# Top-32 attention followed by a SmeLU block: exponentials issued half a step earlier, SmeLU with one read of PSUM, and first products interleaved with the last products of the chunk before

## The chip, the cores and the metric

The kernel runs on one core of a Trainium2 chip. TensorE (PE, with its weight loads as PEld), VectorE (DVE), ScalarE (ACT), GpSimd (POOL) and SyncE (SP, which only issues DMAs here) each work through their own queue of instructions in order, and wait for each other by semaphores. The metric is the device time of one execution in microseconds; lower is better. The kernel before takes 1746.03 us, the median of three runs (1745.57 to 1747.68).

## The reference

All arrays are float32. There are 8 batches, 8 heads, 576 positions and head size 64; the second part has 4608 rows, 512 columns in and out and 2048 hidden columns.

```python
def _attn_ref(q, k, v):
    top_k = 32
    scores = scale * np.matmul(q, k.transpose(0, 1, 3, 2))
    kth = np.partition(scores, -top_k, axis=-1)[..., -top_k:-top_k + 1]
    scores = np.where(scores >= kth, scores, -1000000000.0)
    scores = scores - np.max(scores, axis=-1, keepdims=True)
    attn = np.exp(scores)
    attn = attn / (np.sum(attn, axis=-1, keepdims=True) + 1e-09)
    return np.matmul(attn, v)

def _moe_ref(x, w_in, w_out):          # x: attention output, (B*S, H*D)
    h = x @ w_in
    g = np.where(h >= 1, h, np.where(h <= -1, 0.0, (h + 1) ** 2 / 4.0))
    return g @ w_out
```

## The kernel before

**Steps.** The attention is cut into 144 steps. A step takes 128 query rows for a pair of heads, both held side by side as `[128, 2, 576]` (index `i` below is the head of the pair). In a step:

- `begin` (line 555) has PE make the scores into four PSUM tiles `sp` (line 258), and ACT copies them, scaled, to `s` (line 261). `s` has three buffers.
- `pairs` (line 266): DVE makes `more`, the larger of each score in the first half and its partner in the second, 288 wide.
- `weights` (line 271) finds the 32nd largest score. It is a generator: each `next` emits the instructions up to the next `yield`. DVE takes the eight largest of `more` (`max`, line 283) and strikes them out (`match_replace`, line 292), four times over. After the first eight, ACT forms `nmax`, minus the row maximum, and two exponentials `e` (line 287), one a head. Then DVE handles the smaller partners (lines 297 to 304), makes `more` of the next step (line 309), and masks `e` against the threshold while summing it to `z` (line 312). The reciprocal `rz` (line 318) ends DVE's part, and POOL scales `e` by it (line 325). During the conversion of the weights (the early phase) PE does that scaling with a diagonal matrix instead. `e` has two buffers.
- `transpose_w` (line 333): PE transposes `e` into PSUM and ACT copies it to `wT` (lines 345 and 353). This is one step after the weights were found.
- `values` (line 356): PE multiplies with v, and ACT copies the result into `xT`, the input of the second part. This is another step later.

**Second part.** The 4608 rows form chunks of one or two tiles of 128 rows. For each chunk and each of 16 blocks `f` of 128 hidden columns, `hidden` (line 391) has PE make four accumulating products `ph` (line 394), 128 columns wide for one tile or 256 for two, and the SmeLU gives `g`. In the common path (lines 398 and 412 to 415) ACT reads `ph` twice, `r = Relu(0.5 h + 0.5)` and `g = Relu(h - 1)`, and POOL forms `min(r, 1)`, squares it and adds `g`. There are two buffers of `r`, sixteen of `g`, and three PSUM tiles with the tag `ph`, which `values` uses too. Then `final` (line 417) makes the second products two blocks at a time for one tile into `py` (line 422), and after the last of them ACT copies `py` to `y`, which a DMA writes out. `py` and `y` have one buffer each. The first four chunks of the program handle each tile by itself (128 wide); from the fifth on both tiles go together, where a chunk has two. The last chunk has its own path through DVE (lines 402 to 406).

**Order.** The program writes the order of PE, DVE, ACT and POOL by hand (`tc.manual_schedule`): each engine's instructions stand in the order in which the Python code emits them. The loop at line 605 runs over the steps. In iteration m it emits the values of step m-2 and the scores of step m+2, and then seven slots. `parts` (line 615) says how many `next` of the weights of step m fall into each slot; the transposes of step m-1 come at the end of slot 2 (slot 1 in the early phase); and every slot ends with `advance` (line 501), which emits products of the second part from the queue `pending`, so many that they are spread evenly: `share` (line 611) is the smaller of what is left per step left and what is queued per step until the next chunk is due. The counts are in units of one 128-column product; a `hidden` of two tiles and a pair of `final` count 8 each.

When a chunk's rows are ready, `values_until` (line 587) puts its 16 `hidden` behind what is queued, and its `final` pairs behind those. A second run of the whole program, without the pairing, stands behind a branch that isn't taken here.

## Time and profile before

| | |
|---|---|
| median of three runs | 1746.03 us (1745.57 to 1747.68) |
| the profiled execution | 1746.35 us |
| its span | 1744.5 us |
| mean granted TensorE clock | 0.982 |
| PE matmuls `ph` (line 394) | 3200 records, 558.0 us busy |
| PE matmuls `py` (line 422) | 1152 records, 530.9 us busy |
| DVE maxima (line 283), strikes (line 292) | 465.4 and 375.6 us busy |
| ACT exponentials (line 287) | 288, 213.4 us busy |
| ACT reads of `ph` (lines 398 and 412) | 400 and 368, 166.5 and 153.6 us busy |
| POOL on the products (lines 413, 414, 415) | 173.2, 213.9 and 255.9 us busy |

One matmul of the program is two records in the trace. "Busy" counts the time in which an engine executes at least one instruction; matmuls overlap, so a busy PE isn't necessarily at its fastest, and the distance between the starts of two matmuls that follow each other closely is the better measure of what one costs. A wait in brackets, `[2.00 <-ACT g L412]`, is the idle time of the engine just before the instruction and what ended it. Steps can be counted on DVE by their one reciprocal (line 318).

### The profile page before, as it was taken

The numbers are of one execution on the slowest core, as the hardware profiler recorded it, in microseconds if no ns is written. First come the engines' busy times: TensorE is split into PE (matmuls) and PEld (weight loads), VectorE is DVE, ScalarE is ACT, GpSimd is POOL, SyncE is SP. The second block draws the span as 40 slices with busy tenths as digits, with TensorE's granted clock in tenths as the row PEclk, the third lists the DMA queues.
The fourth block names the chain that finished last, engine by engine and source line by source line (L and its number), as shares of the span: only waits on it lengthen the run. The fifth ranks groups of instructions, "written<-read, shape, count | busy, mean of one in ns | idle before, by whom it ended". The sixth has DMA issues, their size and how long they took to land.

```text
span 1744.5 us, 33535 instructions
## 1 busy us (share of the span) xinstructions
PE 1639.4 (94%) x10665; PEld 1151.5 (66%) x10665; DVE 1537.0 (88%) x4875; ACT 1083.2 (62%) x2942; POOL 946.9 (54%) x1668
## 2 busy tenths in 40 slices
PE   5588989999999999999999999999999999999998
PEld 4476575667766757476756767567667666666665
DVE  7999979888899999999987999999997998899752
ACT  6688575676667857576655647556555555466452
POOL 5689183665544817264646645436365554555550
PEclk7799999999999999999999999999999999999999
DMA  8333112111121112111200101000010000000000
GB/s 253 116 98 97 46 30 65 44 43 41 42 63 52 44 49 65 46 49 41 62 13 22 25 22 44 17 24 17 23 39 19 19 10 14 13 7 7 7 7 15
DMA packets 116668, 74.63 MB, mean 43 GB/s; under 512 B 87296, under 2 KB 95488, under 8 KB 116480
## 3 DMA queue, kind: packets, MB, share of 16 engines
q1 hardware_dynamic: 116480, 72.37, 14.5%
q8 instruction: 87, 1.43, 0.3%
q14 instruction: 101, 0.83, 0.2%
HBM read 62.91 MB, written 9.44 MB: 41 GB/s over the span
## 4 chain that ended last, share of the span: by engine, by line
PE 65%; DVE 14%; POOL 11%; ACT 6%; issue 3%; DMA 0%; POOLq 0%; DVEq 0%; SPq 0%; ACTq 0%
PE py L422 25%; PE ph L394 18%; PE sp L258 7%; PE po L364 7%; PE pw L344 5%; DVE tops L283 4%; DVE more L292 3%; POOL g L415 3%; POOL r L414 3%; DVE e L312 3%; POOL e L325 2%; POOL r L413 2%; ACT s L261 1%; DVE seconds L300 1%; ACT r L398 1%
## 5 line engine op out<-in xcount | busy, mean ns | idle before, releaser
L394 PE MATMUL ph<-xT,w_in 128*128 128x128 f32 (+1 forms) x3200 | 558.0, 326 | 14.4 <-ACT g L412 13.2
L422 PE MATMUL py<-w_out,g 128*128 128x512 f32 x1152 | 530.9, 600 | 2.0 <-ACT y L426 2.0
L394 PEld LDWEIGHTS ph<-xT,w_in 128*128 128x128 f32 x3200 | 472.3, 192 | 87.9 <-ACT g L412 26.0
L325 POOL TENSOR_SCALAR e<-e,rz 128x576 f32<-128x576 f32 x264 | 195.0, 750 | 520.2 <-DVE rz L318 488.8
L283 DVE MAX8 tops<-more 128x8 f32<-128x288 f32 x1152 | 465.4, 445 | 0.0
L292 DVE MATCH_REPLACE8 more<-tops,more 128x288 f32<-128x288 f32 x864 | 375.6, 442 | 0.0
L422 PEld LDWEIGHTS py<-w_out,g 128*128 128x128 f32 x1152 | 205.2, 190 | 224.1 <-issue 215.8
L312 DVE SCALAR_TENSOR_TENSOR e<-s,kth,e 128x576 f32<-128x576 f32 x288 | 245.7, 881 | 116.6 <-ACT e L287 116.3
L398 ACT ACTIVATE r<-ph,half 128x128 f32<-128x128 f32 (+1 forms) x400 | 166.5, 416 | 216.8 <-POOL g L415 156.7
L415 POOL TENSOR_TENSOR g<-r,g 128x128 f32<-128x128 f32 (+1 forms) x384 | 255.9, 666 | 30.2
L413 POOL TENSOR_SCALAR r<-r 128x128 f32<-128x128 f32 (+1 forms) x368 | 173.2, 471 | 132.0 <-ACT r L398 131.7
L414 POOL TENSOR_TENSOR r<-r 128x128 f32<-128x128 f32 (+1 forms) x368 | 213.9, 581 | 30.7
L261 ACT ACTIVATE s<-sp 128x288 f32<-128x288 f32 x576 | 195.2, 421 | 56.8 <-PE sp L258 36.8
L287 ACT ACTIVATE e<-s,nmax 128x576 f32<-128x576 f32 x288 | 213.4, 770 | 7.7
L364 PEld LDWEIGHTS po<-wT,v_in 128*64 128x64 f32 x2048 | 111.8, 137 | 87.9 <-issue 53.2
L258 PE MATMUL sp<-kT,qT 64*128 64x288 f32 x1024 | 163.9, 437 | 4.2 <-ACT kT L218 2.3
L364 PE MATMUL po<-wT,v_in 128*64 128x128 f32 x2048 | 145.5, 280 | 18.7 <-ACT g L412 11.3
L345 ACT COPY wT<-pw 128x512 f32<-128x512 f32 x288 | 154.0, 589 | 13.1 <-PE pw L344 10.6
L344 PEld LDWEIGHTS pw<-ident,e 128*128 128x128 f32 x1056 | 122.2, 142 | 60.0 <-issue 24.4
L344 PE MATMUL pw<-ident,e 128*128 128x128 f32 x1056 | 141.0, 276 | 16.2 <-ACT s L261 10.4
L377 ACT COPY xT<-po 128x128 f32<-128x128 f32 x128 | 34.1, 266 | 195.8 <-PE po L364 195.5
L412 ACT ACTIVATE g<-ph,minus 128x128 f32<-128x128 f32 (+1 forms) x368 | 153.6, 417 | 0.0
(91 smaller groups left out, 1595.1 us busy)
## 6 DMA issues: line engine op xcount, KB each, us to landing
raw<-in_moe_w_out_dram SPq DMA_DIRECT2D x64, 256.0 KB, 2.6
raw<-in_moe_w_in_dram SPq DMA_DIRECT2D x36, 256.0 KB, 2.7
k_in<-in_k_dram SPq DMA_DIRECT2D x64, 128.0 KB, 2.9
q_in<-in_q_dram SPq DMA_DIRECT2D x32, 256.0 KB, 3.1
v_in<-in_v_dram SPq DMA_DIRECT2D x8, 1024.0 KB, 5.8
out_dram<-y SPq DMA_DIRECT2D x32, 256.0 KB, 2.3
kT<-in_moe_w_in_dram SPq DMA_DIRECT2D x16, 256.0 KB, 4.0
v_in<-in_moe_w_in_dram SPq DMA_DIRECT2D x12, 256.0 KB, 4.5
```

Source lines behind the costliest of these rows:

```text
L258: nc.tensor.matmul(o[:, a0 - c0:a1 - c0], qT[d, g, :], kT[d, g, k0:k0 + a1 - a0], start=True, stop=True)
L283: nc.vector.max(out=tops[:, i, r:r + 8], in_=src[:, i, :])
L287: nc.scalar.activation(e[:, i, :], s[:, i, :], AF.Exp, bias=nmax[:, i:i + 1])
L292: nc.vector.match_replace(out=rest[:, i, :], in_to_replace=tops[:, i, r:r + 8], in_values=src[:, i, :], imm_value=LOWEST)
L312: nc.vector.scalar_tensor_tensor(out=e[:, i, :], in0=s[:, i, :], scalar=last[:, i:i + 1], in1=e[:, i, :], op0=ALU.is_ge, op1=ALU.mult, acc ...
L325: nc.gpsimd.tensor_scalar(e[:, i, :], e[:, i, :], rz[:, i:i + 1], 1.0, ALU.mult, ALU.mult)
L344: nc.tensor.transpose(pt[:, c, :], w_in_place, ident)
L364: nc.tensor.matmul(po[j * D:(j + 1) * D], v_in[:, h, c, :] if c < NT else v_tl[0][:, h, :], wT[:, j, c, :] if c < NT else wTt, start=(c == ...
L394: nc.tensor.matmul(ph, w_in[:, kk, f * P:(f + 1) * P], xT[:, kk, c0:c1], start=(kk == 0), stop=(kk == NK - 1))
L414: nc.gpsimd.tensor_tensor(out=r, in0=r, in1=r, op=ALU.mult)
L415: nc.gpsimd.tensor_tensor(out=g, in0=r, in1=g, op=ALU.add)
L422: nc.tensor.matmul(py, gs[f][:, i * P:(i + 1) * P], w_out[:, f, :], start=(f == 0), stop=(f == NF - 1))
```

## The change

Three things change.

1. `pairs`, the first `max`, `nmax` and the exponentials move out of a step's own `weights` into `first_top`, which the step before calls after its last strike and ahead of its last `max`. `weights` of step m therefore begins with a strike and holds the start of step m+1. `parts` is changed to the new count of yields.
2. In the common path of `hidden`, ACT reads `ph` once: `u = Relu(h + 1)` into `g`. POOL forms `c = min(u / 2, 1)` into `r`, then `u - c`, then `c (u - c)`, both in place in `g`. (For u up to 2 this is u²/4, and above it u - 1, which is h.) The path of the last chunk and the path of odd `f` during the conversion keep their operations.
3. From the fifth chunk on, when a chunk becomes ready, up to eight of the last `final` pairs in the queue are taken out and put back with the new chunk's `hidden` spread behind each of them: two `hidden` a pair when there are eight. So that there are such pairs, `share` leaves 64 units in the queue while the next step belongs to a chunk of that kind with two tiles.

```diff
-        def weights(st, after):
-            s, m = st["s"], st["m"]
-            tops = att.tile([P, 2, TOP_K + 8], F32, name="tops", bufs=3)
+        def first_top(st):
+            s = st["s"]
+            if paired:
+                pairs(st)
+            st["tops"] = tops = att.tile([P, 2, TOP_K + 8], F32, name="tops", bufs=3)
             st["e"] = e = att.tile([P, 2, S], F32, name="e")
             nmax = att.tile([P, 2], F32, name="nmax")
+            for i in range(2):
+                nc.vector.max(out=tops[:, i, 0:8], in_=(st["more"] if paired else s)[:, i, :])
+            nc.scalar.activation(nmax, tops[:, :, 0], AF.Copy, scale=-1.0)
+            for i in range(2):
+                nc.scalar.activation(e[:, i, :], s[:, i, :], AF.Exp, bias=nmax[:, i:i + 1])
+                yield
+
+        def weights(st, after):
+            s, m, tops, e = st["s"], st["m"], st["tops"], st["e"]
...
-            for r in range(0, TOP_K, 8):
+            for r in range(8, TOP_K, 8):
+                for i in range(2):
+                    nc.vector.match_replace(out=rest[:, i, :], in_to_replace=tops[:, i, r - 8:r],
+                                            in_values=src[:, i, :], imm_value=LOWEST)
+                src = rest
+                if r == 8:
+                    yield
+                if r + 8 == TOP_K:
+                    yield
+                    yield from first_top(after) if after is not None else (None, None)
                 for i in range(2):
                     nc.vector.max(out=tops[:, i, r:r + 8], in_=src[:, i, :])
-                if r == 0:
-                    nc.scalar.activation(nmax, tops[:, :, 0], AF.Copy, scale=-1.0)
-                    for i in range(2):
-                        nc.scalar.activation(e[:, i, :], s[:, i, :], AF.Exp, bias=nmax[:, i:i + 1])
-                        if i == 0:
-                            yield
-                if r + 8 < TOP_K:
-                    for i in range(2):
-                        nc.vector.match_replace(out=rest[:, i, :], in_to_replace=tops[:, i, r:r + 8],
-                                                in_values=src[:, i, :], imm_value=LOWEST)
-                    src = rest
-                yield
...
-            if paired and after is not None:
-                pairs(after)
...
                 else:
-                    nc.scalar.activation(g, ph, AF.Relu, bias=minus, scale=1.0)
-                    nc.gpsimd.tensor_scalar(r, r, 1.0, 0.0, ALU.min, ALU.max)
-                    nc.gpsimd.tensor_tensor(out=r, in0=r, in1=r, op=ALU.mult)
-                nc.gpsimd.tensor_tensor(out=g, in0=r, in1=g, op=ALU.add)
+                    nc.scalar.activation(g, ph, AF.Relu, bias=one)
+                    nc.gpsimd.tensor_scalar(r, g, 0.5, 1.0, ALU.mult, ALU.min)
+                    nc.gpsimd.tensor_tensor(out=g, in0=g, in1=r, op=ALU.subtract)
+                    nc.gpsimd.tensor_tensor(out=g, in0=g, in1=r, op=ALU.mult)
...
-                    pending.extend(hiddens(i0, i1) + rest + [work for i in range(i0, i1) for work in finals(i)])
+                    new = hiddens(i0, i1)
+                    if i0 == 0 and ch >= EARLY_CHUNKS:
+                        places = []
+                        while pending and not pending[-1][3] and len(places) < NF // 2:
+                            places.append(pending.pop())
+                        for x, work in enumerate(reversed(places)):
+                            pending.append(work)
+                            upto = (x + 1) * NF // len(places)
+                            pending.extend(new[x * NF // len(places):upto])
+                        new = [] if places else new
+                    pending.extend(new + rest + [work for i in range(i0, i1) for work in finals(i)])
...
-            share = min((total - spent) / (n + 2 - m), sum(work[0] for work in pending) / coming)
+            next_chunk = steps[m][3] if m < n else 0
+            keep = NF * DM // P if next_chunk >= EARLY_CHUNKS and len(chunks[next_chunk]) == 2 else 0
+            behind = sum(work[0] for work in pending) - keep
+            share = min((total - spent) / (n + 2 - m), max(behind, 0) / coming)
...
-                parts = [1] * SLOTS if early else [1, 2, 2, 2, 0, 0, 0]
+                parts = [1] * SLOTS if early else [1, 1, 2, 2, 1, 0, 0]
```

PE's transposes of `e` stay as they are. No matmul, DVE instruction or DMA is added or removed.

## The prediction

> **What bounds the kernel now.** I read the page first (its busy row), then busy time by stage, then the waits of the whole run and of each stage, then one crowded step in order of time.
>
> ```profile
> PE 1639.4 (94%) x10665; PEld 1151.5 (66%) x10665; DVE 1537.0 (88%) x4875; ACT 1083.2 (62%) x2942; POOL 946.9 (54%) x1668
> ```
>
> Two engines are near full, and neither is full all the time. Busy time by stage (the window in us, its length, then each engine) shows that they take turns:
>
> ```profile
> 160.00:345.00 185.00, 172.47 (x1199) 119.71 (x1198) 160.19 (x519) 119.57 (x352) 103.04 (x212) 1.00 0.17 51
> 345.00:510.00 165.00, 157.39 (x1162) 113.19 (x1162) 140.80 (x460) 108.95 (x324) 87.81 (x188) 0.99 0.17 48
> 510.00:895.00 385.00, 372.45 (x2371) 259.56 (x2370) 373.17 (x1191) 266.23 (x733) 212.11 (x347) 1.00 0.17 48
> 895.00:1062.00 167.00, 163.45 (x991) 110.08 (x990) 143.53 (x457) 93.57 (x239) 76.21 (x137) 1.00 0.09 22
> 1252.00:1531.00 279.00, 276.69 (x1772) 193.21 (x1771) 241.87 (x762) 159.98 (x405) 156.62 (x261) 0.99 0.07 18
> 1605.00:1692.00 87.00, 83.11 (x493) 59.09 (x492) 63.04 (x198) 42.34 (x114) 55.16 (x100) 1.00 0.02 7
> ```
>
> DVE is full in 510-895 (97%); PE is in 1252-1531 (99%); in 160-510 neither is. The waits say why (who waited for whom: us, times, longest):
>
> ```profile
> ACT r L398 <- POOL g L415: 156.7, 113, 6.4
> POOL r L413 <- ACT r L398: 131.7, 46, 10.0
> DVE e L312 <- ACT e L287: 116.3, 80, 6.3
> ```
>
> DVE's only large wait is for the exponentials. Asked by stage, that row is 41.1 us in 160-510, 1.9 in 510-895, 19.6 in 895-1062, 0.7 in 1062-1252, 30.6 in 1252-1531 and 22.3 after 1605: it lies where DVE is not full. One crowded step, from the timeline:
>
> ```profile
> 322.14 1.09 PE L364 MATMUL po<-wT,v_in 128*64 128x128 f32 x16 [2.00 <-ACT g L412]
> ...
> 321.47 0.37 ACT L398 ACTIVATE r<-ph,half 128x128 f32<-128x128 f32 x1 [2.30 <-POOL g L415]
> 321.73 0.36 ACT L412 ACTIVATE g<-ph,minus 128x128 f32<-128x128 f32 x1
> 323.14 0.37 ACT L398 ACTIVATE r<-ph,half 128x128 f32<-128x128 f32 x1 [1.05 <-POOL g L415]
> ...
> 326.55 0.78 ACT L287 ACTIVATE e<-s,nmax 128x576 f32<-128x576 f32 x1
> ...
> 327.36 0.82 DVE L312 SCALAR_TENSOR_TENSOR e<-s,kth,e 128x576 f32<-128x576 f32 x1 [4.56 <-ACT e L287]
> ```
>
> One chain stops three engines. ACT writes `r` into one of two buffers, so it may not be more than two products ahead of POOL; POOL needs about 1.3 us a product (its adds into `g` begin at 323.93, 325.21 and 326.49); ACT stands, PE stands behind the PSUM tile (2.00 us), and the exponential queued behind on ACT makes DVE stand (4.56 us).
>
> **Floors.** A DVE step without POOL work lasts 10.18 us (reciprocals at 1210.61 and 1220.79). PE issues a 512-column `py` every 0.429 us (12 in 5.15 on the chain), a 256-column `ph` every 0.216 (16 in 3.46), a 128-column one every 0.112 (128 in 14.29). The step 1312.3-1324.5 has PE busy throughout and 20 to 21 `py` (8.6-9.0 us), so attention costs PE 3.2-3.6 us a step; I take 3.5. In 160-510 (30 steps, 256 `py`, 817 narrow `ph`) PE needs 109.8 + 91.5 + 105 = 306 us and DVE 305 plus what POOL costs it; the stage lasts 350. So some 40 us are lost to the chain above. In 895-1062 PE needs 60.5 + 31.1 + 14.3 + 49 = 155 of 167 (141 `py`, 144 wide and 128 narrow `ph`, 14 steps); in 1252-1531 it is 87.1 + 80.8 + 14.3 + 84 = 266 of 279 (203, 374, 128, 24 steps).
>
> **The change part by part.**
>
> *smelu.* Outside the last chunk and the odd `f` of the weight-conversion phase, 368 products lose one ACT read of PSUM: 192 narrow at 369 ns and 176 wide at 470 ns, 154 us of ACT. ACT is no bound (62%), so the relief alone is worth nothing. What counts is that ACT no longer writes `r`: its one `Relu` goes to `g`, which has 16 buffers. The wait of ACT for POOL (156.7 us) has nothing left to wait for. What is late next is POOL itself: it still does three operations a product, and the squaring (697 ns wide, 475 narrow) becomes an operation of two tensors like the add (817, 539), so 176 x 0.12 + 192 x 0.064 = 33 us more POOL work. That stays beside other work while POOL's lag is under the time between an `e` scaling and its transposes. In a step of eight narrow products POOL needs 8 x 1.47 + 1.7 = 13.5 us against DVE's 11, a lag of 2.5 us; the products of three such steps, 16 x 1.47 + 3 x 1.7 = 29 us, fit in 33. So POOL isn't a bound over three steps.
>
> *Exponentials sooner.* `first_top` puts `pairs`, the first maxima, `nmax` and both exponentials of step m+1 before the last maxima of step m: no instruction is added. Before, DVE stood as soon as ACT was some 4 us late; now the exponentials have a whole step, about 10 us. That covers the longest wait seen, 6.3 us, so I let the row of 116.3 us go; what appears instead is PE, where PE is the bound.
>
> *A wait added.* `e` has two buffers, and in the new order ACT's exponential of m+1 stands ahead of the copies of m-1's transposes, so it waits for PE's transposes of m-1, and before that `nmax` waits for DVE's maxima, some 6 us into the step. Behind it on ACT: two `wT` copies, the `Relu` of slots 2 to 6, `y` copies; PE waits for those only after three PSUM tiles, 3 x 1.73 = 5.2 us. ACT resumes at about 6.3 + 0.2 + 1.5 + 1.5 = 9.5 us of the step; PE's transposes end about 5 to 7 us into it (in the step begun at 1210.9, the copies that follow them start at 1218.15). I take nothing; between 0 and 0.5 us on some 100 steps (0 and +50).
>
> *Interleaving and the reserve.* From the fifth chunk on, a chunk's 16 wide products go two by two between the last eight `final` pairs of the chunk before. PE's instructions are the same in number. DVE loses to POOL wherever both work: `more` takes 740 ns in 605-646 and 1052 in 1177-1200, the masking 813 and 1051. The same work is spread over more steps, and `pairs` moves to where POOL is busy: +4, between -8 and +15. `keep` holds 64 units back, and in the orders of both programs the changed one has issued 13.7 us fewer products up to the transposes of step 124. They were taken from a stretch where DVE is the bound (steps 36-43) and fall into the last 20 steps, where PE mostly is: +12, between +5 and +14.
>
> *DMAs.* None is added. With the interleaved `final` pairs the copies of `y` and their output DMAs (median 2.3 us to landing) come later on ACT's and SP's queues, past loads of keys, queries and weight pieces, which have whole steps of cover; DMA is 1 to 3 tenths busy after the start. Nothing; were that cover gone, 2 to 3 us at each of 32 outputs' landings that something waits for, of which `y`'s rows show 0.7 us.
>
> The page "SBUF — State Buffer", section "Who interferes with whom", of the Trainium skill speaks against the change: a VectorE instruction with two SBUF inputs and a GpSimd one that reads SBUF exclude each other for the whole instruction. The rows show +0.31 us for `more`, not a whole 0.73 us POOL operation. By the rule some 85 steps of `pairs` would cost +0.73 each where 16 us are paid now, about +46 instead of +4.
>
> **Sum.** Stage 160-510: of 40 us lost, 24 come back (DVE's waits there are 41.1, but POOL's 13.5 us steps keep some; between 8 and 38). 895-1062 and 1252-1531: 25 us above PE's need, half of it, 12 (0 to 25). Where PE's stages meet DVE's, DVE may now be some 7 us further ahead; three such changes, and part of it, 6 (0 to 20). Early stage (30-160: DVE busy 128.2 of 130), 510-895 and the tail after 1692: nothing, since DVE's own work, then the last chunk's unchanged path, fill them (-3 to +3). -24 - 12 - 6 + 12 + 4 = -26 on the profiled span of 1744.5, 1718.5; the execution took 1746.35, 1.85 more than its span, and stands 0.3 over the median 1746.03. So 1720.
>
> **Rivals.** *Much faster*: the chain is undone wholly and the regimes average out; 38 + 25 + 20 saved against 12 + 4: 1679 to 1700. For: PE's and DVE's needs in 160-510 are near 306. Against: uneven steps remain, some with 12 us of products. *Smaller gain or none*: POOL paces 160-510 all the same (busy 13.5 us of the crowded steps), only 8 come back there and 6 elsewhere, and the 12 come late: 1736 to 1750. For: POOL's row of 131.7 us waiting for ACT is small beside its work in these steps. *Slower*: ACT's new hold stalls PE. Its place is the `Relu` and `y` copies behind the exponential; it decides from the point where PE's transposes end earlier than 9.5 - 5.2 = 4.3 us into a DVE step. At 0.2 us a step over 130 steps (26 us) the gain is gone; at 0.5, 65 - 26 gives 1785. Against: a PE that falls behind by 2 us no longer meets the hold, as DVE is then ahead.
>
> **How the numbers follow.** Forecast with 1700 to 1736: 0.58; much faster 0.12; smaller gain (1736 to 1742.5) 0.12; no change, within 0.2% (3.5 us, what a measurement of this kernel can tell) 0.06; slower 0.12. Faster 0.82, same 0.06, slower 0.12. The range runs from 1692, inside the much faster case, to 1747, and leaves out some 0.05 below and 0.14 above. The forecast's own range is 1700 to 1736.
>
> **What would show it.** Right: no row of ACT waiting for POOL's `g`; DVE's wait for `e` under 20 us; ACT near 930 us busy, POOL near 980; the stage up to step 40 shorter by 20 us or more; the last 20 steps longer by some 10. Wrong: PE's waits for ACT's `g`, `y` or `wT` growing by tens of us with ACT standing at `nmax` or `e`; PE waiting for POOL's `e`; DVE steps without products over 10.3 us.

## The result, and the profile after

The changed kernel takes 1756.5 us, the median of four runs (1755.72 to 1758.43), beside 1746.04 us (1745.57 to 1747.68) for the kernel before on the same chip. The ratio is 1.006, with a 95% interval of 1.0042 to 1.0077: slower by 0.6%, where the prediction had 1720 and faster. The profiled execution has a span of 1756.6 us. The busy row of its page:

```profile
PE 1646.4 (94%) x10665; PEld 1161.7 (66%) x10665; DVE 1580.9 (90%) x4875; ACT 974.0 (55%) x2574; POOL 1196.7 (68%) x1669
```

ACT was to be near 930 us and is at 974; POOL was to be near 980 and is at 1197. The groups of POOL's instructions, with shapes kept apart (count, then busy us, mean ns of one, idle before and what ended it), say where that is. Before:

```profile
L413 POOL TENSOR_SCALAR r<-r 128x256 f32<-128x256 f32 x176 | 98.6, 560 | 65.1 <-ACT r L398 64.8
L413 POOL TENSOR_SCALAR r<-r 128x128 f32<-128x128 f32 x192 | 74.6, 389 | 66.9 <-ACT r L398 66.9
```

After:

```profile
L424 POOL TENSOR_SCALAR r<-g 128x256 f32<-128x256 f32 x176 | 210.3, 1195 | 98.9 <-ACT g L423 70.4 <-ACT nmax L283 21.3 <-PE py L433 7.1
L425 POOL TENSOR_TENSOR g<-g,r 128x256 f32<-128x256 f32 x176 | 146.5, 833 | 14.7
L426 POOL TENSOR_TENSOR g<-g,r 128x256 f32<-128x256 f32 x176 | 159.1, 904 | 13.8
L424 POOL TENSOR_SCALAR r<-g 128x128 f32<-128x128 f32 x192 | 142.7, 743 | 105.3 <-ACT g L423 87.9 <-ACT nmax L283 17.5
```

The clamp is an operation of the same kind on the same shape, and takes twice as long: 1195 ns in place of 560, 743 in place of 389. That is 179.8 us more on POOL. A wide product now costs POOL 1.19 + 0.83 + 0.90 = 2.93 us (2.07 before), a narrow one 1.81 (1.40).

The stages in the windows of before:

```profile
160.00:345.00 185.00, 170.62 (x1198) 121.36 (x1198) 167.46 (x529) 108.01 (x303) 116.89 (x198) 0.97 0.18 52
345.00:510.00 165.00, 152.73 (x1117) 109.67 (x1113) 142.20 (x444) 95.73 (x270) 125.78 (x210) 0.98 0.16 45
...
895.00:1062.00 167.00, 167.00 (x1035) 114.48 (x1033) 161.85 (x494) 86.54 (x218) 122.81 (x161) 1.00 0.08 22
1252.00:1531.00 279.00, 277.26 (x1795) 194.51 (x1793) 259.42 (x787) 137.81 (x341) 211.16 (x263) 1.00 0.07 19
```

In 160-510, where a gain of 24 us was expected, PE is now less busy than before (323 us of 350 against 330). In 895-1062 PE and DVE are busier together than before (167 and 162 against 163 and 144): that stage did improve. The waits of the whole run:

```profile
POOL e L335 <- DVE rz L328: 188.0, 44, 8.9
...
POOL r L424 <- ACT g L423: 158.3, 46, 13.6
ACT nmax L283 <- DVE tops L282: 154.0, 61, 5.3
...
ACT e L285 <- PE pwt L362: 102.6, 72, 7.8
...
DVE more L271 <- ACT s L263: 48.3, 25, 7.0
PEld pw L354 <- POOL e L335: 46.5, 39, 6.2
```

The two rows that the prediction wanted gone are all but gone: of ACT's waits for POOL's `g`, 156.7 us at the reads of `ph` before, 3.9 us are left there (in the path that keeps its operations) and 9.0 stand at the exponentials, and DVE waits for the exponentials 5.0 us in place of 116.3. Three came in their place. PE's weight loads wait for POOL's scaled `e`, ACT's exponential waits for PE's transposes, and DVE waits for ACT's scores. In the timeline they follow one another (start, length, engine, line; the wait in brackets):

```profile
278.38 1.47 POOL L335 TENSOR_SCALAR e<-e,rz 128x576 f32<-128x576 f32 x2
279.18 1.97 PE L354 MATMUL pw<-ident,e 128*128 128x128 f32 x8 [6.01 <-POOL e L335]
...
280.94 0.42 PE L362 MATMUL pwt<-ident,e 128*128 128x128 f32 x1
...
281.48 1.44 ACT L285 ACTIVATE e<-s,nmax 128x576 f32<-128x576 f32 x2 [7.82 <-PE pwt L362]
...
291.62 0.76 DVE L271 TENSOR_TENSOR more<-s 128x576 f32<-128x576 f32 x1 [3.04 <-ACT s L263]
```

POOL comes to the scaling of `e` late, behind its products; PE stands 6.0 us until it is done; ACT stands 7.8 us at the next exponential, because one of the two `e` is still being transposed. Some 10 us later DVE stands 3.0 us, waiting for ACT's scores.

Where the time went, step range by step range: the time between the reciprocals of DVE (one a step), summed, and from the last reciprocal to the end of the span. Rows named by what they are; they are explained below.

| us | 0-10 | 11-39 | 40-75 | 76-89 | 90-107 | 108-130 | 131-143 | rest | span |
|---|---|---|---|---|---|---|---|---|---|
| before | 160.5 | 347.2 | 385.0 | 168.7 | 191.0 | 278.5 | 161.1 | 52.5 | 1744.5 |
| after | 166.7 | 346.9 | 394.8 | 155.0 | 197.8 | 270.1 | 159.0 | 66.5 | 1756.6 |
| after, fast clamp | 164.6 | 327.6 | 388.0 | 154.6 | 195.1 | 275.1 | 159.6 | 62.9 | 1727.6 |
| after, no reserve | 166.9 | 348.3 | 398.5 | 169.7 | 200.0 | 289.0 | 159.8 | 63.0 | 1795.2 |
| before, slow clamp | 162.2 | 360.5 | 403.8 | 172.2 | 198.5 | 299.9 | 167.4 | 63.7 | 1828.2 |
| before, fast clamp | 160.7 | 328.7 | 389.6 | 160.8 | 194.6 | 270.3 | 154.8 | 57.6 | 1717.1 |
| 16-bit c | 160.2 | 336.4 | 383.8 | 162.9 | 191.6 | 271.0 | 158.3 | 53.1 | 1717.1 |
| 16-bit c, spread | 160.2 | 336.6 | 382.3 | 162.1 | 191.6 | 271.2 | 152.3 | 52.3 | 1708.6 |
| 16-bit c, spread, sooner | 163.5 | 333.7 | 388.1 | 158.3 | 196.4 | 265.1 | 153.8 | 61.5 | 1720.4 |
| the same, `pairs` earlier | 163.5 | 334.6 | 383.4 | 160.6 | 192.5 | 265.7 | 153.1 | 61.3 | 1714.7 |

From before to after, steps 76-89 and 108-130 gave 22.1 us; steps 0-10, 40-75, 90-107 and the rest lost 6.2 + 9.8 + 6.8 + 14.0. Steps 11-39 gave nothing.

This table counts at DVE, and where the exponentials come sooner DVE runs further ahead of PE: from its last reciprocal to PE's last transpose `pwt` it is 6.9 us before and 20.3 after. So time moves from one of its columns to another without being won or lost. The order of PE's transposes was not changed. Counted from the start of one step's `pwt` to that of another, and from the last one to the end, the same traces give:

| us | 0-10 | 11-39 | 40-75 | 76-89 | 90-107 | 108-130 | 131-143 | rest |
|---|---|---|---|---|---|---|---|---|
| before | 163.8 | 349.6 | 388.6 | 167.0 | 194.5 | 275.0 | 160.2 | 45.8 |
| after | 169.1 | 352.0 | 392.1 | 162.1 | 193.5 | 274.5 | 167.0 | 46.3 |
| after, fast clamp | 167.0 | 330.6 | 391.3 | 162.1 | 192.4 | 274.5 | 164.8 | 45.0 |
| the same, no reserve | 167.0 | 336.5 | 387.6 | 163.9 | 192.4 | 272.4 | 153.1 | 44.9 |
| before, fast clamp | 163.8 | 330.6 | 389.8 | 163.0 | 193.5 | 271.4 | 158.5 | 46.5 |
| 16-bit c | 163.4 | 338.5 | 385.1 | 163.8 | 190.7 | 271.8 | 158.0 | 45.8 |
| 16-bit c, spread | 163.5 | 337.0 | 385.3 | 163.1 | 190.5 | 272.4 | 151.7 | 45.0 |
| 16-bit c, spread, sooner | 166.0 | 342.3 | 386.0 | 163.9 | 191.3 | 272.4 | 153.4 | 45.2 |
| the same, `pairs` earlier | 166.0 | 342.7 | 383.4 | 163.9 | 188.0 | 272.4 | 153.3 | 44.9 |

Here steps 76-89 and 108-130 gave 5.4 us from before to after, steps 0-10, 11-39, 40-75 and 131-143 lost 5.3 + 2.4 + 3.5 + 6.8, and the time after the last transpose stayed (45.8 and 46.3).

### The profile page after: what moved, and what is told of

It reads as the page before. It is cut to its first block, busy times and chain, and to the rows that moved or that the text cites. A ratio compares the mean times of both kernels' runs of the same rounds, so it can differ in the third digit from the quotient of the medians.

```text
span 1756.6 us, 32761 instructions
## 1 busy us (share of the span) xinstructions
PE 1646.4 (94%) x10665; PEld 1161.7 (66%) x10665; DVE 1580.9 (90%) x4875; ACT 974.0 (55%) x2574; POOL 1196.7 (68%) x1669
## 4 chain that ended last, share of the span: by engine, by line
PE 48%; DVE 33%; POOL 11%; issue 5%; ACT 2%; DMA 1%; DVEq 0%; POOLq 0%; ACTq 0%
PE py L433 18%; PE ph L404 14%; DVE more L298 8%; DVE tops L307 7%; PE sp L260 5%; PE po L374 5%; POOL r L424 4%; DVE e L322 4%; PE pw L354 4%; POOL g L426 3%; DVE seconds L312 3%; DVE more L309 3%; POOL g L425 3%; DVE more L271 2%; DVE tops L282 2%
## 5 line engine op out<-in xcount | busy, mean ns | idle before, releaser
L433 PE MATMUL py<-w_out,g 128*128 128x512 f32 x1152 | 541.1, 603 | 4.6 <-ACT y L437 4.6
L404 PEld LDWEIGHTS ph<-xT,w_in 128*128 128x128 f32 x3200 | 478.2, 193 | 101.4 <-issue 54.7
L424 POOL TENSOR_SCALAR r<-g 128x128 f32<-128x128 f32 (+1 forms) x368 | 353.0, 959 | 204.2 <-ACT g L423 158.3
L307 DVE MAX8 tops<-more 128x8 f32<-128x288 f32 x864 | 349.1, 445 | 0.0
L335 POOL TENSOR_SCALAR e<-e,rz 128x576 f32<-128x576 f32 x264 | 205.8, 790 | 206.7 <-DVE rz L328 188.0
L433 PEld LDWEIGHTS py<-w_out,g 128*128 128x128 f32 x1152 | 205.7, 192 | 207.9 <-issue 194.3
L426 POOL TENSOR_TENSOR g<-g,r 128x128 f32<-128x128 f32 (+1 forms) x368 | 265.4, 721 | 28.8
L285 ACT ACTIVATE e<-s,nmax 128x576 f32<-128x576 f32 x288 | 208.8, 768 | 126.1 <-PE pwt L362 102.6
L425 POOL TENSOR_TENSOR g<-g,r 128x128 f32<-128x128 f32 (+1 forms) x368 | 244.6, 665 | 30.7
L322 DVE SCALAR_TENSOR_TENSOR e<-s,kth,e 128x576 f32<-128x576 f32 x288 | 255.8, 925 | 9.9 <-ACT e L285 5.0
L423 ACT ACTIVATE g<-ph,one 128x128 f32<-128x128 f32 (+1 forms) x368 | 151.5, 425 | 182.4 <-PE ph L404 181.9
L263 ACT ACTIVATE s<-sp 128x288 f32<-128x288 f32 x576 | 195.1, 416 | 57.1 <-PE sp L260 51.2
L354 PEld LDWEIGHTS pw<-ident,e 128*128 128x128 f32 x1056 | 122.1, 142 | 76.5 <-POOL e L335 46.5
L271 DVE TENSOR_TENSOR more<-s 128x576 f32<-128x576 f32 x144 | 120.1, 834 | 48.4 <-ACT s L263 48.3
L312 DVE MAX8 seconds<-more 128x8 f32<-128x288 f32 x288 | 118.3, 452 | 20.3 <-POOL excess L337 6.6
```

The costliest lines, as they stand in the source:

```text
L285: nc.scalar.activation(e[:, i, :], s[:, i, :], AF.Exp, bias=nmax[:, i:i + 1])
L307: nc.vector.max(out=tops[:, i, r:r + 8], in_=src[:, i, :])
L322: nc.vector.scalar_tensor_tensor(out=e[:, i, :], in0=s[:, i, :], scalar=last[:, i:i + 1], in1=e[:, i, :], op0=ALU.is_ge, op1=ALU.mult, acc ...
L354: nc.tensor.transpose(pt[:, c, :], w_in_place, ident)
L404: nc.tensor.matmul(ph, w_in[:, kk, f * P:(f + 1) * P], xT[:, kk, c0:c1], start=(kk == 0), stop=(kk == NK - 1))
L424: nc.gpsimd.tensor_scalar(r, g, 0.5, 1.0, ALU.mult, ALU.min)
```

## The experiments

Each time stands beside the kernel before on the same chip, which took 1744.4 to 1746.0 us (medians). In the texts on record, Theory A is that GpSimd's new pair of operations is slow by itself, B that the other tile or contention makes it slow, C that VectorE's own new order and the products put off carry the loss.

### What makes the clamp slow

```diff
-                    nc.gpsimd.tensor_scalar(r, g, 0.5, 1.0, ALU.mult, ALU.min)
+                    (one of eight pairs of operations, by f % 8, the rest as changed)
```

> The changed kernel, but POOL's tensor_scalar from g to r takes one of eight pairs of operations, by f modulo 8 (0: times 0.5, min 1, as changed; 1: min 2, times 0.5; 2: min 2, max 0; 3: times 0.5, times 1; 4: min 2 alone; 5: times 0.5 alone; 6: max 0, min 2; 7: times 0.5, max 0), so most of its g are other numbers. Theory A (the pair of operations sets POOL's speed, not the other tile or the traffic): 0 stays at the 1195 ns wide and 743 narrow that the changed kernel shows, and at least 2 comes near the 560 and 389 of the old pair min, max. Theory B (reading g and writing r, or more contention with DVE, is what costs): all eight lie within 15% of each other, near 1195 and 743.

One run, 1742.2 us. The groups of its `TENSOR_SCALAR`, 128x256 alone. L425 is mult 0.5 then min 1, L427 min 2 then mult 0.5, L433 min alone, L435 mult alone, L429 min 2 then max 0, L431 mult 0.5 then mult 1:

```profile
L427 POOL TENSOR_SCALAR r<-g 128x256 f32<-128x256 f32 x22 | 27.1, 1231 | 4.5 <-ACT g L423 4.1 <-ACT nmax L283 0.4
...
L425 POOL TENSOR_SCALAR r<-g 128x256 f32<-128x256 f32 x22 | 24.8, 1127 | 72.0 <-ACT g L423 52.2 <-ACT nmax L283 19.8
...
L435 POOL TENSOR_SCALAR r<-g 128x256 f32<-128x256 f32 x22 | 21.0, 955 | 15.7 <-ACT g L423 14.3 <-ACT nmax L283 1.5
L433 POOL TENSOR_SCALAR r<-g 128x256 f32<-128x256 f32 x22 | 19.3, 877 | 10.5 <-ACT nmax L283 8.5 <-ACT g L423 2.0
...
L431 POOL TENSOR_SCALAR r<-g 128x256 f32<-128x256 f32 x22 | 11.5, 523 | 13.5 <-ACT g L423 13.5
L429 POOL TENSOR_SCALAR r<-g 128x256 f32<-128x256 f32 x22 | 11.3, 515 | 2.8 <-ACT g L423 2.8
```

Same tiles, same neighbours, same engine: only the pair differs. (These are means, and they include waits for the neighbours; the shortest ones, on 128x128, are 286 to 292 ns for the two fast pairs, 521 and 524 for one operation alone, and 637 to 647 for the other pairs.) Min then max, and mult then mult, take 515 and 523 ns; every other pair tried (max then min too, 1163) takes 1127 to 1328, and even one operation alone takes 877 or 955. Theory A holds and B falls. The kernel before has a fast pair in its clamp (min 1, max 0).

The price of that in the changed kernel, with the clamp made min(u, 1) by the fast pair. Every kernel with this "fast clamp" leaves out the half, so it computes another function; the instructions and their order stay:

```diff
-                    nc.gpsimd.tensor_scalar(r, g, 0.5, 1.0, ALU.mult, ALU.min)
+                    nc.gpsimd.tensor_scalar(r, g, 1.0, 0.0, ALU.min, ALU.max)
```

> The changed kernel with POOL's old pair of operations, min 1 and max 0, from g to r: c becomes min(u, 1) and the output differs; all instructions and their order stay. Theory A (the slow POOL operation ate the gain, 180 us of POOL): 1756.5 falls by 15 to 30, to 1727 to 1742. Theory C (DVE's own order, 0.26 us a step, and the products put off are the loss): within 5 us of 1756.5. POOL's busy time falls from 1197 to about 1010 in both.

1729.35 us (1727.65 to 1732.5), ratio 0.9921 (0.9904 to 0.9937); POOL 989 us busy. So the slow pair costs the changed kernel some 24 to 27 us (by the ratios and by the times) and turns a gain into a loss. Steps 11-39 shrink from 346.9 to 327.6 us, 19.6 below the 347.2 of before: most of the prediction's 24 us are there, and 19.3 of them hung on this operation.

### The parts one by one

VectorE's own order: `pairs` of the next step moved ahead of the last strike, so that the first maxima no longer follow it at once.

```diff
             for r in range(8, TOP_K, 8):
+                if paired and r + 8 == TOP_K and after is not None:
+                    pairs(after)
                 for i in range(2):
                     nc.vector.match_replace(
```

> The changed kernel with the pairs of the next step one instruction group earlier on DVE, ahead of the last strike instead of behind it, so that the first maxima don't follow directly on the pairs they read. Theory C (a DVE instruction that reads what the one just before it wrote waits some 0.13 us, and the new order has two such places a step more): the step without POOL work falls from 10.44 to 10.31, and the time by 8 to 15 us, as more than half of the 144 steps are DVE's. Theory A alone: the step falls as well, but the time by less than 5, since POOL and PE pace the rest.

1753.97 us (1749.95 to 1754.22), ratio 1.006 (1.0043 to 1.0077), the same ratio as the changed kernel. The floor of a step without products went from 10.44 to 10.30 us as Theory C said, and steps 40-75 from 394.8 to 391.4, so the effect is real; it is too small to carry the loss, and far from the 8 to 15 us of Theory C.

The change with the old SmeLU (two reads, squaring) put back:

```diff
-                    nc.scalar.activation(g, ph, AF.Relu, bias=one)
-                    nc.gpsimd.tensor_scalar(r, g, 0.5, 1.0, ALU.mult, ALU.min)
-                    nc.gpsimd.tensor_tensor(out=g, in0=g, in1=r, op=ALU.subtract)
-                    nc.gpsimd.tensor_tensor(out=g, in0=g, in1=r, op=ALU.mult)
+                    (the five lines of before)
```

> The changed kernel with the old SmeLU (two ACT reads, min and max, square, add): the sooner exponentials and the interleaving alone. Theory A (the new SmeLU costs more than it gives): faster than the changed kernel, 1735 to 1750. Theory C: the old SmeLU's hold of ACT by POOL comes back on top of DVE's slower step and the products put off: 1756 to 1775.

1744.43 us (1742.57 to 1745.61), ratio 1.0 (0.9991 to 1.001). Without the new SmeLU the rest of the change is worth nothing, though DVE's wait for the exponentials is gone there as well: it waits 78.8 us for the scores instead.

The other way round, the kernel before with the new SmeLU alone, slow and fast:

> The kernel before with the new smelu alone (one PSUM read, then mult 0.5 and min 1 in one GpSimd operation, subtract, mult); exponentials and order of products as before. Theory A (the new smelu carries the loss through its slow GpSimd operation, whatever the order): 1752 to 1768 us, GpSimd near 1200 us busy. Rival F (the slow operation hurts only because the sooner exponentials make GpSimd's scalings of e urgent): 1742 to 1748 us, as before.

> The kernel before with the one-read smelu whose clamp is the fast pair (c = min(u, 1), output differs); exponentials and order of products as before. Theory A with the prediction's mechanism (ScalarE freed of the two buffers of r is the gain, mostly): 1726 to 1734 us, ScalarE's wait for GpSimd gone, VectorE's wait for the exponentials under 60 us. Rival H (the gain needs the exponentials half a step sooner as well, since a block of products still stands ahead of them): 1738 to 1746 us, with VectorE's wait for the exponentials near the 116 us of before.

Slow: 1831.93 us (1830.36 to 1834.96), ratio 1.0506 (1.0489 to 1.0524), far above what Theory A had written down. Fast: 1720.01 (1719.43 to 1721.36), ratio 0.9862 (0.9845 to 0.9878), better than Theory A's 1726 to 1734; DVE's wait for the exponentials is 61.2 us. The one-read SmeLU by itself, with a fast clamp, gives all that was forecast of the whole change, and one pair of operations moves that kernel by 112 us, over four times what it moves the changed kernel. What happens in the slow one, from its timeline:

```profile
1462.17 1.07 POOL L416 TENSOR_SCALAR r<-g 128x256 f32<-128x256 f32 x1
1463.33 1.17 POOL L417 TENSOR_TENSOR g<-g,r 128x256 f32<-128x256 f32 x1
1464.58 1.12 POOL L418 TENSOR_TENSOR g<-g,r 128x256 f32<-128x256 f32 x1
1465.68 1.47 POOL L327 TENSOR_SCALAR e<-e,rz 128x576 f32<-128x576 f32 x2
...
1478.50 1.47 POOL L327 TENSOR_SCALAR e<-e,rz 128x576 f32<-128x576 f32 x2
...
1466.48 1.85 PE L346 MATMUL pw<-ident,e 128*128 128x128 f32 x8 [3.36 <-POOL e L327]
...
1467.51 0.59 ACT L347 COPY wT<-pw 128x512 f32<-128x512 f32 x1 [3.48 <-PE pw L346]
...
1479.24 1.34 DVE L314 SCALAR_TENSOR_TENSOR e<-s,kth,e 128x576 f32<-128x576 f32 x1 [4.75 <-ACT e L289]
```

POOL runs without a gap, takes 2.6 to 3.5 us a product, and comes to `e` when PE's transposes are already due: PE stands, ACT stands behind PE, and by the next step DVE stands behind ACT. With four wide products in a step (4 x 2.81 us by the means of this kernel, and 1.6 for `e`) POOL needs 12.8 us, which is also the distance of its two scalings of `e` above (1465.68 and 1478.50). In the kernel before, most steps with four wide products last 11.37 or 11.38 us. With the fast clamp POOL needs 10.4. The pair lifts POOL over the length of a step, and from there on POOL sets the pace.

Is it that time as such, or something else the slow pair does? The fast clamp, done twice:

```diff
                     nc.gpsimd.tensor_scalar(r, g, 1.0, 0.0, ALU.min, ALU.max)
+                    nc.gpsimd.tensor_scalar(r, r, 1.0, 0.0, ALU.min, ALU.max)
```

> The kernel before with the one-read smelu and the fast clamp (c = min(u, 1), output differs), the clamp done twice, the second time from r to r: one more fast GpSimd operation a product, about 560 ns wide and 390 narrow, against the 635 and 354 by which the slow pair is longer. With one clamp it took 1720.0 us, with the slow pair 1831.9. Theory N (GpSimd's time as such is what costs, by pacing the crowded steps): 1800 to 1840 us. Rival O (the slow operation does something beyond its own time, to VectorE or to ScalarE): 1725 to 1770 us.

1830.84 us (1829.96 to 1832.29), ratio 1.0485 (1.0469 to 1.0501): the same loss with two fast operations, 515 + 472 ns wide and 380 + 349 narrow:

```profile
L416 POOL TENSOR_SCALAR r<-g 128x256 f32<-128x256 f32 x176 | 90.6, 515 | 71.7 <-ACT g L415 71.7
L417 POOL TENSOR_SCALAR r<-r 128x256 f32<-128x256 f32 x176 | 83.0, 472 | 14.8
```

It is POOL's time. Theory N holds.

Why then does the changed kernel lose only 10 us? Its reserve and its spreading taken out, first with the fast clamp, then with the slow one as changed:

```diff
-            keep = NF * DM // P if next_chunk >= EARLY_CHUNKS and len(chunks[next_chunk]) == 2 else 0
+            keep = 0
```

```diff
-                    if i0 == 0 and ch >= EARLY_CHUNKS:
+                    if False:
```

> The changed kernel with c = min(u, 1) through the fast pair (min 1, max 0), so its output differs, and without the reserve: keep = 0, so that products are handed out as in the kernel before. To be compared with the same kernel with the reserve, 1729.35 us, whose end after the last reciprocal was 62.9 us long against 52.5 us before the change. Theory D (the reserve puts products off into the last steps, where TensorE is the bound, and costs what the prediction said, 5 to 14 us): 1715 to 1724 us; the end back at 53 to 57 us. Rival E (the products put off come out of steps where VectorE is the bound, so that what the end gains those steps lose, or the long end has another cause): 1726 to 1733 us.

> The same kernel (c = min(u, 1), output differs, keep = 0) and also without the spreading of a chunk's first products among the last ones of the chunk before: they are queued in one block again. Theory D holds the spreading for nearly free of cost: within 4 us of the kernel that only loses the reserve. Rival G (the crowded blocks are what ScalarE and GpSimd choke on, so the spreading is where the gain comes from): 8 us or more slower than that kernel.

> The changed kernel without the reserve (keep = 0), everything else as changed, the slow operation included. Theory D (the reserve puts products into the last steps, and that costs the same 10 us whatever the smelu): 1744 to 1750 us, so no change to the kernel before. Rival I (with the slow operation GpSimd paces the crowded steps, and products put off relieve them): 1752 to 1762 us.

> The changed kernel without the reserve and without the spreading: the new smelu with its slow operation and the sooner exponentials alone. The new smelu alone took 1831.9 us. Theory J (the exponentials half a step sooner are what takes most of that loss back, since VectorE no longer waits for a ScalarE that is late behind GpSimd): 1748 to 1768 us. Rival K (it is the spreading that takes it back, by parting GpSimd's blocks of products): 1785 to 1835 us.

| us (ratio, 95%) | fast clamp, min(u, 1) | slow clamp, as changed |
|---|---|---|
| new SmeLU alone | 1720.0 (0.9845 to 0.9878) | 1831.9 (1.0489 to 1.0524) |
| + exponentials sooner | 1725.4 (0.9869 to 0.9902) | 1830.7 (1.0472 to 1.0507) |
| + spreading | 1719.8 (0.9840 to 0.9873) | 1795.2 (1.0260 to 1.0312) |
| + reserve (the whole change) | 1729.4 (0.9904 to 0.9937) | 1756.5 (1.0042 to 1.0077) |

With a fast clamp Theory D is right about the size: the reserve costs 9.6 us, though the end after the last reciprocal didn't go back to 53 to 57 us (60.7). The spreading is worth 5.6 there, more than Theory D's 4 and less than Rival G's 8. With the slow one it is wrong by its sign: the reserve gains 38.7 us and the spreading 35.4, because POOL is what they relieve. In the changed kernel the steps 108 to 112 last 11.05, 11.05, 11.50, 11.50 and 11.50 us; without the reserve 11.29, 11.32, 11.74, 16.77 and 12.91. By the code, fewer second products are then left in the queue for a new chunk to be spread among. Theory J is wrong as well, and Rival K right: the sooner exponentials take back nothing (1831.9 and 1830.7). Where DVE waited for the exponentials 172 us, it now waits for the scores 92 us, ACT's exponentials wait for PE's transposes 232 us, and PE's loads for POOL's `e` 113 us: the same lateness of POOL, passed on through other waits.

### A version that keeps the gain

The gain of the one-read SmeLU was put down to ACT's lead over POOL. A second way to that lead keeps both reads: `c` in 16 bits (bf16), so that the two buffers of `r` hold four halves, and the clamp is a fast pair on the finished `c`. An error of c enters c(u - c) only squared below u = 2, since the product is largest at c = u/2. (Of the edit, the lines of the other two paths, which keep their operations, are not shown.)

```diff
-                    nc.scalar.activation(r, ph, AF.Relu, bias=half, scale=0.5)
-                    nc.scalar.activation(g, ph, AF.Relu, bias=minus, scale=1.0)
-                    nc.gpsimd.tensor_scalar(r, r, 1.0, 0.0, ALU.min, ALU.max)
-                    nc.gpsimd.tensor_tensor(out=r, in0=r, in1=r, op=ALU.mult)
-                nc.gpsimd.tensor_tensor(out=g, in0=r, in1=g, op=ALU.add)
+                    if not halves:
+                        two_c = pool.tile([P, CW], F32, name="r", bufs=2).bitcast(BF16)
+                        halves.extend([two_c[:, CW:2 * CW], two_c[:, 0:CW]])
+                    c = halves.pop()[:, 0:c1 - c0]
+                    nc.scalar.activation(c, ph, AF.Relu, bias=half, scale=0.5)
+                    nc.scalar.activation(g, ph, AF.Relu, bias=one)
+                    nc.gpsimd.tensor_scalar(c, c, 1.0, 0.0, ALU.min, ALU.max)
+                    nc.gpsimd.tensor_tensor(out=g, in0=g, in1=c, op=ALU.subtract)
+                    nc.gpsimd.tensor_tensor(out=g, in0=g, in1=c, op=ALU.mult)
```

> The kernel before (its exponentials, its order) with c(u - c) from two PSUM reads: ScalarE writes c = relu(x/2 + 1/2) in 16 bits, four halves in the place of the two buffers of r, and u = relu(x + 1) to g; GpSimd takes the fast pair (min 1, max 0) on c, then subtracts and multiplies in 32 bits. Everything is computed. Theory L (what the fast one-read smelu gained, 24.5 us, is ScalarE's freedom to run ahead of GpSimd; four buffers give most of it, and the second PSUM read costs nothing): 1722 to 1732 us, ScalarE's wait for GpSimd under 40 us, ScalarE near 1140 us busy. Rival M (the operations with a 16-bit operand are slow on GpSimd, or the second read matters): 1740 to 1780 us.

1718.80 us (1717.38 to 1719.09), ratio 0.9842 (0.9825 to 0.9858), better than Theory L had it, though ACT's wait for POOL is 63.6 us where it had under 40. And with only one half of each buffer used, which takes the lead away and leaves the operations:

> The kernel before with the 16-bit c of the last runs, but only one half of each buffer used, so ScalarE may again be two products ahead of GpSimd and not four; operations unchanged, everything is computed. With four it took 1718.8 us. Theory L (the lead is the gain): 1735 to 1748 us, ScalarE's wait for GpSimd back above 120 us. Rival P (the gain comes from the other operations or the narrower type): 1717 to 1726 us.

1745.84 us (1745.25 to 1747.27), ratio 1.0001 (0.9992 to 1.001). The waits, with four halves:

```profile
DVE e L315 <- ACT e L290: 84.2, 65, 6.3
...
ACT r L421 <- POOL g L425: 63.6, 45, 4.0
```

and with two:

```profile
ACT r L421 <- POOL g L425: 153.9, 111, 6.4
DVE e L315 <- ACT e L290: 113.6, 78, 6.3
```

The second is the picture of before (156.7 and 116.3), and the time is that of before. So the lead is the gain, and the operations and the type are worth nothing either way. The second read takes nothing that can be seen from the whole: with it and four halves 1718.8 us, without it and with the fast clamp 1720.0. In 11-39 the four halves bring 10.8 us, the fast one-read form 18.5; whether that is more lead or the missing read wasn't told apart.

The same SmeLU in the changed order without the reserve, then in the order of before with the spreading alone, then in the changed order with `pairs` ahead of the last strike:

> The same smelu in the changed kernel's order without the reserve (exponentials sooner, products spread). Everything is computed. Theory L: 1720 to 1732 us, within 5 us of the same smelu in the order before, since with the fast clamp both orders took 1720 us. Rival M: 1735 to 1760 us.

> The kernel before with the 16-bit c in four halves, and a chunk's first products spread among the last ones of the chunk before; exponentials as before, no reserve; everything is computed. Theory Q (spreading is worth 5 us with a fast GpSimd, the sooner exponentials cost 5): 1711 to 1716 us. Rival R (spreading helps only because the sooner exponentials hold ScalarE): 1717 to 1722 us.

> The changed order without the reserve and with the 16-bit c in four halves (1722.2 us), and pairs put before the last strike, so that the first maxima do not follow it at once; everything is computed. Theory Q with the bubbles of VectorE as the price of the sooner exponentials: steps without products 10.30 us long in place of 10.44, some 60 such steps and more that VectorE paces, 1712 to 1718 us. Rival S (the price is ScalarE's hold, not the bubbles): 1720 to 1724 us.

| 16-bit c, four halves | us (lowest to highest) | ratio, 95% |
|---|---|---|
| order of before | 1718.80 (1717.38 to 1719.09) | 0.9842 (0.9825 to 0.9858) |
| and spreading | 1710.59 (1710.03 to 1711.22) | 0.9796 (0.9782 to 0.9809) |
| and exponentials sooner | 1722.17 (1720.44 to 1722.37) | 0.9861 (0.9844 to 0.9877) |
| and `pairs` ahead of the last strike | 1717.65 (1716.27 to 1720.56) | 0.9838 (0.9825 to 0.9852) |

The best kernel is the one with the new SmeLU and the spreading and without the sooner exponentials: 2.0% faster than before and 2.6% faster than the changed kernel. Spreading gives 8 us even without them, so Rival R falls; most of it lies in steps 131-143 (158.0 and 151.7 us, counted at PE). The sooner exponentials cost some 11 us. Part of that is DVE's own: steps 40-75, where DVE is full, take 382.3 us without and 388.1 with them, and 383.4 with `pairs` moved (counted at PE 385.3, 386.0 and 383.4). The changed kernel's timeline of a step without products shows why:

```profile
754.80 0.45 DVE L298 MATCH_REPLACE8 more<-tops,more 128x288 f32<-128x288 f32 x1
755.16 0.76 DVE L271 TENSOR_TENSOR more<-s 128x576 f32<-128x576 f32 x1
755.95 0.82 DVE L282 MAX8 tops<-more 128x8 f32<-128x288 f32 x2
756.68 0.80 DVE L307 MAX8 tops<-more 128x8 f32<-128x288 f32 x2
...
759.45 0.24 DVE L316 MAX8 kth<-tops 128x8 f32<-128x9 f32 x2
759.72 0.82 DVE L322 SCALAR_TENSOR_TENSOR e<-s,kth,e 128x576 f32<-128x576 f32 x1
```

and the same place with `pairs` moved:

```profile
702.30 0.81 DVE L308 MAX8 tops<-more 128x8 f32<-128x288 f32 x2
703.02 0.74 DVE L272 TENSOR_TENSOR more<-s 128x576 f32<-128x576 f32 x1
703.68 0.08 DVE L299 MATCH_VALUE_LOAD more<-tops,more 128x8 f32 x1
```

and `pairs` (L269) in the kernel before:

```profile
1218.17 0.24 DVE L304 MAX8 kth<-tops 128x8 f32<-128x9 f32 x2
1218.33 0.74 DVE L269 TENSOR_TENSOR more<-s 128x576 f32<-128x576 f32 x1
1218.99 0.81 DVE L312 SCALAR_TENSOR_TENSOR e<-s,kth,e 128x576 f32<-128x576 f32 x1
```

An instruction that doesn't need the one before starts 0.08 to 0.09 us before that one's end (755.16 against 755.25, 703.02 against 703.11); one that does starts about 0.03 us after it (755.95 against 755.92, 759.72 against 759.69). Before, `pairs` stood between `kth` and the masking and filled that gap. The change opened it and made a second one between `pairs` and the first maxima: 10.18 us a step became 10.44. Moving `pairs` closes one of them (10.31), and 36 steps at 0.13 us are 4.7 us, which is what steps 40-75 gained at DVE; the whole kernel gained 4.5 (1722.17 to 1717.65). So that share of the cost is shown. Counted at DVE, the time after step 130 grows by 10.7 us (204.6 without the sooner exponentials, 215.3 with), but that is mostly DVE's greater lead: counted at PE it grows by 1.9 (196.7 and 198.6), and 7.8 of the 11.8 us lie in steps 0-39 (500.5 and 508.3). What causes them there wasn't tried. (With the exponentials goes the changed hand-out of the weights to the slots, which wasn't tried by itself.)

## Why the prediction was wrong

**The step that failed is the cost of the SmeLU on POOL.** The prediction priced what becomes of the squaring (33 us more for POOL) and let the clamp stand at the 560 and 389 ns of its row of before, without a word on its operations. Kind, shape and engine are the same; the pair of operations differs, and it made 1195 and 743 of them (the run with eight pairs tells this from the change of tiles: min then max takes 515 ns on the same ones). The condition that the prediction wrote down shows how near the edge it stood: three steps with 16 narrow products fit in 33 us at 1.47 us a product (29 us). At the measured 1.81 they take 34. "POOL isn't a bound over three steps" became false by that row alone. The rival "POOL paces 160-510 all the same" is what happened, with 0.3 us coming back there, fewer than its 8.

The measured sign is that of the rival "slower", but not for its reason, ACT's hold: with the slow clamp the kernel takes 1831.9 us without the sooner exponentials and 1830.7 with them.

- **-24 in 160-510**: right in its mechanism and near in size, as soon as the clamp is fast: -19.6 us in steps 11-39 of the changed kernel, -18.5 with the SmeLU alone. Undoing the lead undoes the gain. Nearly all of it came from ACT's lead, not from the exponentials. That the SmeLU alone, with the fast clamp, takes the very 1720 us of the forecast is chance; the whole change with it takes 1729.4.
- **-12 in 895-1062 and 1252-1531**: about half is there. The 22.1 us that steps 76-89 and 108-130 gave are mostly DVE's greater lead; counted at PE it is 5.4, and 7.6 with the fast one-read SmeLU alone, so it needs neither spreading nor reserve.
- **-6 where stages meet**: little of it; steps 90-107 lost 6.8 us counted at DVE, and gave 1.0 counted at PE (2.1 with the fast clamp).
- **The exponentials sooner, "no instruction is added"**: true, and yet not free. The order opened two gaps on DVE, 0.26 us in a step without products. The prediction's own sign for being wrong, steps over 10.3 us without products, showed it.
- **+12 for the reserve**: 9.6 us with the fast clamp. With the slow one it gains 38.7: the sign of this term depended on POOL. The place was right: with the fast clamp steps 131-143 take, at PE, 164.8 us with the reserve and 153.1 without. The 14.0 us by which the time after DVE's last reciprocal grew are mostly something else, DVE's lead, and are there without the reserve too (60.7 and 63.0 us against 52.5).
- **+4 for contention, against +46** by the rule of the Trainium skill, page "SBUF — State Buffer", section "Who interferes with whom": the rows of `pairs` stand at 853 ns before and 834 after, those of the masking at 881 and 925. That is some 10 us over all steps, nearer to the +4. The traces show who waits, and for how long. In the kernel before, one `pairs` started while POOL was adding, and took 1.05 us in place of the 0.74 of an undisturbed one; the clamp that POOL began next took 0.85 in place of 0.40:

```profile
1011.10 0.72 POOL L415 TENSOR_TENSOR g<-r,g 128x256 f32<-128x256 f32 x1
1011.39 1.05 DVE L269 TENSOR_TENSOR more<-s 128x576 f32<-128x576 f32 x1
1011.86 0.85 POOL L413 TENSOR_SCALAR r<-r 128x256 f32<-128x256 f32 x1
```

The extra 0.31 us of `pairs` is less than the 0.43 that was left of the add, and the clamp's 0.45 less than the 0.58 that was left of `pairs`. That agrees with the page, where the two exclude each other and the later one waits for the earlier one to finish. The +46 charged a whole operation of POOL's in each of 85 steps, where the wait is only for what is left of one.

- **ACT's hold, taken as nothing (0 to 50)**: it is there (102.6 us of ACT waiting for `pwt`), started by POOL's late `e`, not by ACT. With fast clamps it remains at about 100 us and goes with 1720 us, so most of it seems to be time that ACT has; this is argued, not tested.
- **The early stage, taken as nothing (-3 to +3)**: steps 0-10 lost 6.2 us, and 3.0 to 4.1 with fast clamps and the sooner exponentials.

## What to carry to other kernels

Take a duration from a row only if the operations agree too, not just the kind of instruction, the shape and the engine; where they differ, the row is one end of a range. Then compare what an engine off the critical path needs per step with the length of a step: in steps with four wide products POOL went from 10.4 to 12.8 us, where such a step lasted 11.4 before, and that crossing, not its 57 or 64% of the span, decided 112 us. And when one engine's events mark the steps, look whether that engine runs further ahead of the others in one of the two kernels; here DVE's lead over PE at the last step grew from 6.9 to 20.3 us. When buffers limit how far one engine runs ahead of another, halving the element size of a buffer can double the lead without a byte more.

## What the runs showed of the hardware

- GpSimd's `TENSOR_SCALAR` on f32 depends on the pair of operations: on 128x256 it took 515 to 523 ns for min-max and mult-mult, 877 to 955 ns for a single min or mult, and 1127 to 1328 ns for mult-min, min-mult, max-min and mult-max. Taking the second operation away makes a fast pair slower.
- On VectorE an instruction that needs the result just before it cost 0.11 to 0.13 us more than one that doesn't. The Trainium skill, on the page "VectorE: DVE Perf Modes", section "The DRAIN you can't avoid", reports of eight copies in a row that a semaphore after each of them costs nothing extra, and adds that an instruction that isn't held starts earlier. For the instructions here the need for the result does cost: the steps of 10.18, 10.31 and 10.44 us have none, one and two such places more. What lies between two dependent instructions is worth choosing, though here it was worth only some 5 us.
- On 16-bit `c` the fast pair took 563 ns on 128x256, as on 32 bits (560): the narrower type bought room, not time (in that operation).
